# Spreading a block's operand splits by due time, and preparing the second part's first block inside the first part

## The chip, the cores and the metric

The kernel runs on one core of one Trainium2 chip. The metric is the time of one execution on the device in microseconds. The core has five engines with instruction queues of their own: TensorE (PE, with its weight loads as PEld), VectorE (DVE), ScalarE (ACT), GpSimd (POOL) and SyncE (SP, which here only issues DMAs). DMAs can be issued from SP's, ScalarE's and POOL's queue.

## The reference, cut to what matters

```python
# q, k, v: 8 batches x 8 heads x 576 tokens x 64, fp32; k and v are pooled by 8 along the tokens
k_p, v_p = mean over 8 tokens of k, v                   # 72 keys per head
attn = softmax(q @ k_p.T / 8);  o = attn @ v_p          # 8 x 8 x 576 x 64
x = o.transpose(0, 2, 1, 3).reshape(4608, 512)
h = x @ w_in                                            # 512 -> 2048
g = h if h >= 1, 0 if h <= -1, else (h + 1)**2 / 4
x2 = g @ w_out                                          # 2048 -> 512
h = x2 @ w_in2                                          # 512 -> 2048
out = (h - tanh(h)) @ w_out2                            # 2048 -> 512, out is 4608 x 512
```

Each fp32 matrix is cut into a high part, rounded to TensorE's fp32r, and a low part, the remainder. A product is the sum of three: high by high, low by high, high by low. "A split" below is the pair of instructions that makes both parts: ScalarE copies the high part, VectorE subtracts it from the source for the low part.

## The kernel before, in words

The program has two parts.

**Part 1** does the attention and the first layer, in 12 blocks of 384 tokens. Each block has 16 steps (one for each 128 of the 2048 columns). In a step TensorE does the h products of step t and the output products of step t-2; ScalarE and VectorE compute g and split it. Between them stand the pieces of the attention for the next block: queries times keys, the softmax, its transposition (`at_pe`), the copies of the transposed probabilities from PSUM (`at_evac`, `at_evac_a`) and the product with the values (`pv`, L547 to L550). A plan (`add(t, slot, fn)`) says at which step a piece stands in the program; the framework's scheduler then orders each engine's instructions by readiness, with program order as priority. The pooled sequence has 72 keys, 64 + 8 per head: `ah` and `al` hold the 64 of two heads (128 rows), and the remainders of 8 go to `ar`. `at_evac_a` copies them, for each of the block's three token tiles, as one piece of 32 rows (L521) and one of 16 rows (L522). The plan also prepares the second layer's weights (`w2_conv`, `w2_sums`, `w2_own`, `w2_mixed`, 16 units, one per 128 columns): converted, combined into the sums that part 2 needs (four on POOL, L241 to L250), split (L253 on ScalarE, L254 on VectorE) and written to DRAM as `w2c` and `w2o`. Part 1's output goes to DRAM as `x2d`, with stores at L645: on SP's queue, those of the last block on ScalarE's.

**Part 2** does the second layer by Strassen-Winograd: 2 x 2 quarters of each matrix and 7 products in place of 8. It runs over 5 blocks J of 768, 1024, 1024, 1024 and 768 tokens. For each block there are 8 pairs of column tiles q; for each the 7 h products (`h_prod`, L966, order 1, 6, 7, 2, 5, 4, 3, into banks bkA, bkX and bkZ) are combined by VectorE (v_w L995, v_t L998, c22 L1002, c21 L1006, c12 L1009), ScalarE takes tanh (L1013), and g = h - tanh(h) is made in halves by POOL and VectorE (L1017). Two pairs form a group k; the group's operands for the output products are sums of g (`g_s1` to `g_s4`, POOL, L1028 to L1039), split by ScalarE (L1049) and VectorE (L1054). Seven output products (`o_prod`, L1071) follow 8 products behind the h's, VectorE adds each to an accumulator (L1095), and POOL folds the accumulators at a block's end (L1108). The x operands of a block are loaded (`xr_load`, L919), four of the seven are differences (`x_t1` to `x_t4`, POOL, L943 to L953), and all seven are split (`xc_hi` L936 on ScalarE, `xc_lo` L940 on VectorE). The weights come by `wq_load` (L901, nine buffers) and `wo_load` (L906, four buffers) on SP's queue.

In part 2 each engine's order is fixed by hand: `at_time(t, fn, ...)` gives each step a planned time (us, 0 at part 2's first product), computed by a small model of TensorE's time (`ended` of an h product, `began` of an output product), and the steps are emitted in order of these times. The planned times only set the order; what runs when is decided by semaphores. Negative times stand before part 2's first product.

Part 2's buffers lie over part 1's in the same SBUF, slot by slot (`LAYOUT`). A new buffer is placed in the instruction order only after the whole pool of part 1 beneath it is done. Slot r3 (one of the x operands) lay over `sb`, the work buffers that part 1 uses to its last instruction; `half`, a constant of the g computation, lay in the pool `const` with buffers that are done much earlier.

Of the kernel before, what the change touches and what calls it, by code (L numbers as in the profile page):

```python
# [51 lines left out]
def attention_two_moe_kernel(  # L52
# [35 lines left out]
    const = one_pool("const")  # L88
    wpa = one_pool("wpa")
# [18 lines left out]
    ident = const.tile([P, P], F32, tag="ident", name="ident")  # L108
    half = const.tile([P, 1], F32, tag="half", name="half")
    mask = const.tile([P, 2], F32, tag="mask", name="mask")  # L110

    third = const.tile([P, 16], F32, tag="third", name="third")[:, 0:1]
# [398 lines left out]
    def at_evac_a(j, p):  # L511
# [6 lines left out]
        else:  # L518
            for i in range(NTI):
                c = slice(i * P, (i + 1) * P)  # L520
                nc.scalar.activation(ar_t[0:32, c], pr[32 * i : 32 * i + 32], AF.Copy)  # L521
                nc.vector.tensor_copy(ar_t[32:48, c], pr[32 * i : 32 * i + NR])  # L522
# [114 lines left out]
    def out_evac(j):  # L637
        ost = sb.tile([P, KC * TB], F32, tag="ost", name="ost", bufs=1)
        for c in range(KC):
# [5 lines left out]
            (nc.sync if j < NB - 1 else nc.scalar).dma_start(out=x2d[j][c], in_=o)  # L645
# [173 lines left out]
    for f in range(FC):  # L819
# [7 lines left out]
        add(t + 2, "w", w2_sums, f)  # L827
        add(t + 4, "w", w2_own, f)
# [35 lines left out]
    for x in (ps_a, ps_h, ps_o):  # L864
# [11 lines left out]
        "q0 q1 q2 q3 q4 q5 q6 p1664 o0 o1 g0 s0 q7 q8 p2048 x1 x6 r4 o2 o3 r3 g1 k0 k1 th s1 p1024"  # L876
# [64 lines left out]

    def x_t1(J):
        nc.gpsimd.tensor_tensor(XR[(J, 0)], XR[(J, 3)], XR[(J, 0)], ALU.subtract)  # L943

    def x_t3(J):
        nc.gpsimd.tensor_tensor(XR[(J, 3)], XR[(J, 2)], XR[(J, 3)], ALU.subtract)

    def x_t2(J):
        XR[(J, 4)] = two("r4", [P, 2, M2], F32, "xr")[:, :, 0 : half(J)]
        nc.gpsimd.tensor_tensor(XR[(J, 4)], XR[(J, 2)], XR[(J, 0)], ALU.subtract)  # L950

    def x_t4(J):
        nc.gpsimd.tensor_tensor(XR[(J, 1)], XR[(J, 1)], x_src(J, 6), ALU.subtract)  # L953
# [72 lines left out]

    def g_s1(k):
        nc.gpsimd.tensor_tensor(u_of(k, 1), a_of(k, 0, 1), a_of(k, 1, 1), ALU.add)  # L1028

    def g_s2(k):  # L1030
        nc.gpsimd.tensor_tensor(u_of(k, 2), u_of(k, 1), a_of(k, 0, 0), ALU.subtract)  # L1031

    def g_s3(k):
        a = a_of(k, 0, 1)
        nc.gpsimd.tensor_tensor(a, a_of(k, 0, 0), a, ALU.subtract)

    def g_s4(k):
        a = a_of(k, 1, 0)
        nc.gpsimd.tensor_tensor(a, a, u_of(k, 2), ALU.subtract)  # L1039
# [90 lines left out]
    now, ended, began, slots = 0.0, {}, {}, []  # L1130
    LAG = 8
    for s in range(7 * NG + LAG):
        if s < 7 * NG:
            J = s // (7 * NGR)
            for i in (2 * s, 2 * s + 1):
                at_time(now, h_prod, i)
                now += 6 * half(J) * 0.000454
                ended[i] = now
        for n in [s - LAG] if s > LAG + 2 else {LAG + 1: [0], LAG + 2: [1, 2]}.get(s, []):
            k = n // 7  # L1140
            now = max(now, split_at(n) + 2.5)
            at_time(now, o_prod, n)
            began[n] = now
            now += 6 * (half(k // NGR) // P) * 0.1185
            at_time(now + 0.1, add_up, n)
    for i in range(14 * NG):
        at_time((-60 if i < 7 else -18) + i if i < NQ else ended[i - NQ] + 0.05, wq_load, i)
    for n in range(7 * NG):
        at_time((-55 + n, -55 + n, -26, -25)[(n + 2) % 4] if n < NO else began[n - NO] + 3, wo_load, n)
# [5 lines left out]
    for q in range(2 * NG):  # L1155
# [12 lines left out]
        if q % 2:  # L1168
# [6 lines left out]
            at_time(t + 8.1 * r if k == NG - 1 else max(t + 8.1 * r, began[7 * k + 2]), g_s4, k)  # L1175
    for J in range(NJ):
# [4 lines left out]
        steps = (  # L1181
            (e[1], xc_hi, 1), (e[1] + 1.1, xc_lo, 1),
            (e[1] + 2.6, x_t1), (e[1] + 5.2, x_t2), (e[1] + 7.8, x_t3),
            (max(e[6], e[1] + 7.9), xc_hi, 6), (max(e[6], e[1] + 7.9) + 1.1, xc_lo, 6),
# [47 lines left out]
```

## Time and profile before

| what | value |
|---|---|
| median of 3 runs | 1802.79 us (1800.83 to 1806.29) |
| profiled execution | 1803.29 us, span 1801.5 us |
| mean granted TensorE clock | 0.982 |
| TensorE busy | 1705.1 us, 95% |
| VectorE busy | 1240.5 us, 69% |
| ScalarE busy | 844.5 us, 47% |
| POOL busy | 706.2 us, 39% |

The span runs from the first to the last instruction of the profiled execution. Part 1 fills it up to 1015.6 us, when the first matmul of L966 starts; part 2 is the rest. Busy time is that of instructions that compute; a TensorE that is busy at clock 0.5 does half as much. The four block switches of part 2 lie around 1130, 1286, 1454 and 1624 us.

### The profile page before, as it was taken

The page shows a single profiled execution, that of the slowest core. Times are in us where ns is not written, and L with a number is a line of the kernel's source. Part 1 is how long each engine was busy: PE and PEld are TensorE (multiplying, and loading weights), DVE is VectorE, ACT ScalarE, POOL GpSimd, SP SyncE. Part 2 cuts the span into 40 slices and gives each one's busy share as a digit, 9 for nine tenths or more (in the row PEclk, how much of TensorE's full clock was granted, in tenths as well). Part 3 has the DMA queues.
Part 4 walks back from the last instruction along what each step waited for, and adds up shares of the span by engine and source line. Part 5 has one row for each costly group of instructions (what it writes and reads, how often), then busy time and mean ns, then how long its engine had stood idle before and what let it go on. Part 6 is the DMA issues. An engine that isn't in the chain of part 4 may idle for free. (4 is left out here: it accounts for less than half of the span.)

```text
span 1801.5 us, 28136 instructions
## 1 busy us (share of the span) xinstructions
PE 1705.1 (95%) x10176; PEld 1591.5 (88%) x10176; DVE 1240.5 (69%) x1797; ACT 844.5 (47%) x1842; POOL 706.2 (39%) x589
## 2 busy tenths in 40 slices
PE   8999989999989999899999899899899989998997
PEld 6569989899989999898999899799789978998996
DVE  8877766666757676766554457856875787578575
ACT  6656545455545455555443344353435344433442
POOL 5441243321434322432001045644564466446344
PEclk9999999999999999999999999999999999998999
DMA  8631243523434233433101478577556756664873
GB/s 253 224 105 31 68 144 94 150 63 110 136 101 123 89 120 91 144 97 102 27 27 44 154 230 291 171 227 234 167 182 210 234 153 219 199 209 149 285 228 123
DMA packets 220538, 270.56 MB, mean 150 GB/s; under 512 B 82672, under 2 KB 152304, under 8 KB 220400
## 3 DMA queue, kind: packets, MB, share of 16 engines
q1 hardware_dynamic: 219824, 267.98, 47.6%
q8 instruction: 81, 1.33, 0.3%
q10 hardware_dynamic: 576, 0.79, 0.1%
q14 instruction: 57, 0.47, 0.1%
HBM read 219.94 MB, written 48.23 MB: 149 GB/s over the span
## 5 line engine op out<-in xcount | busy, mean ns | idle before, releaser
L1071 PEld LDWEIGHTS ob<-wo,sp 128*128 128x128 f32 x3024 | 384.9, 193 | 32.8 <-DVE sp L1054 16.0
L1071 PE MATMUL ob<-wo,sp 128*128 128x256 f32 x3024 | 392.4, 285 | 20.8 <-DVE sp L1054 13.0
L601 ACT ACTIVATE g<-g,half 128x384 f32<-128x384 f32 x192 | 118.7, 618 | 219.7 <-DVE g L597 219.0
L1017 POOL TENSOR_TENSOR g<-g,th 128x1024 f32<-128x1024 f32 (+1 forms) x40 | 91.7, 2293 | 311.5 <-ACT th L1013 204.6
L635 PE MATMUL po<-gh,whl 128*128 128x384 f32 x704 | 200.0, 345 | 0.0
L966 PE MATMUL bkX<-xc,wq 128*128 128x512 f32 (+1 forms) x720 | 175.4, 380 | 25.1 <-DVE g L1009 15.4
L590 PE MATMUL ph<-xh,whl 128*128 128x384 f32 x704 | 197.0, 341 | 0.8 <-DVE g L605 0.8
L614 DVE TENSOR_TENSOR gl<-g,gh 128x384 fp32r<-128x384 f32 x176 | 118.1, 671 | 77.7 <-ACT gh L613 75.3
L966 PEld LDWEIGHTS bkX<-xc,wq 128*128 128x128 f32 x720 | 131.2, 193 | 44.7 <-DVE g L1009 17.4
L1054 DVE TENSOR_TENSOR sp<-g,sp 128x1024 fp32r<-128x1024 f32 (+1 forms) x100 | 149.8, 1498 | 27.1 <-ACT sp L1049 27.1
L1013 ACT ACTIVATE th<-g 128x1024 f32<-128x1024 f32 (+1 forms) x80 | 78.0, 975 | 191.2 <-DVE g L1006 112.8
L605 DVE TENSOR_TENSOR g<-ph,g 128x384 f32<-128x384 f32 x192 | 106.7, 556 | 81.0 <-ACT g L601 80.0
L478 POOL TENSOR_TENSOR ex<-ex,rc 128x432 f32<-128x432 f32 x44 | 44.0, 999 | 301.8 <-DVE rc L473 154.6
L597 DVE TENSOR_SCALAR g<-ph 128x384 f32<-128x384 f32 x192 | 106.0, 552 | 64.7 <-PE ph L590 58.4
L1095 DVE TENSOR_TENSOR ac<-ob,ac 128x1024 f32<-128x1024 f32 (+1 forms) x110 | 122.2, 1111 | 35.2 <-PE ob L1071 34.9
L613 ACT ACTIVATE gh<-g 128x384 fp32r<-128x384 f32 x176 | 91.5, 520 | 100.8 <-PE po L635 53.7
L1049 ACT ACTIVATE sp<-g 128x1024 fp32r<-128x1024 f32 (+1 forms) x100 | 97.0, 970 | 81.6 <-PE ob L1071 49.2
L635 PEld LDWEIGHTS po<-gh,whl 128*128 128x128 f32 x704 | 131.7, 192 | 0.0
L590 PEld LDWEIGHTS ph<-xh,whl 128*128 128x128 f32 x704 | 128.6, 188 | 2.0 <-DVE g L605 1.7
L590 PE MATMUL ph<-xh,wh 128*128 128x384 f32 x352 | 121.0, 344 | 4.4 <-DVE g L605 4.4
L635 PE MATMUL po<-gh,wh 128*128 128x384 f32 x352 | 123.0, 350 | 0.0
L635 PE MATMUL po<-gl,wh 128*128 128x384 f32 x352 | 121.4, 345 | 0.0
(166 smaller groups left out, 3878.8 us busy)
## 6 DMA issues: line engine op xcount, KB each, us to landing
wq<-w2c SPq DMA_DIRECT2D x280, 256.0 KB, 3.6
wo<-w2o SPq DMA_DIRECT2D x140, 512.0 KB, 3.6
wraw<-in_moe_w_in_dram SPq DMA_DIRECT2D x32, 512.0 KB, 4.0
wraw<-in_moe_w_out_dram SPq DMA_DIRECT2D x32, 512.0 KB, 4.7
out_dram<-ac SPq DMA_DIRECT2D x72, 128.0 KB, 1.8
x2d<-ost SPq DMA_DIRECT2D x44, 192.0 KB, 1.9
w2c<-wraw SPq DMA_DIRECT2D x16, 512.0 KB, 2.9
w2o<-wraw SPq DMA_DIRECT2D x16, 512.0 KB, 2.8
```

Source lines behind the costliest of these rows:

```text
L590: nc.tensor.matmul(ps, a[:, cs], x[:, c, :], start=(i == 0), stop=(i == 3 * KC - 1))
L597: nc.vector.tensor_scalar(a, hp[t], -1.0, 1.0, ALU.max, ALU.min)
L601: nc.scalar.activation(a, a, AF.Square, bias=half, scale=0.5)
L605: nc.vector.tensor_tensor(a, hp.pop(t), a, ALU.max)
L614: nc.vector.tensor_tensor(gl, a, gh.bitcast(F32), ALU.subtract)
L635: nc.tensor.matmul(o, a, m, start=(f == 0 and i == 0), stop=(f == FC - 1 and i == len(ops) - 1))
L966: nc.tensor.matmul(o, w[:, wi, c], x[:, xi, c], start=new and n == 0, stop=n == 5, skip_group_check=not new)
L1017: eng.tensor_tensor(g_of(q, i), g_of(q, i), SN.pop((q, i)), ALU.subtract)
L1049: nc.scalar.activation(x[:, 0, :, 0 : half(k // NGR)], o_src(k, OORD[mi]), AF.Copy)
L1054: nc.vector.tensor_tensor(x[:, 1], o_src(k, OORD[mi]), x[:, 0].bitcast(F32), ALU.subtract)
L1071: nc.tensor.matmul(o[:, c], x[:, xi, p, c * P : (c + 1) * P], w[:, p, wi], start=new and first, stop=True, skip_group_check=not (new and f ...
L1095: nc.vector.tensor_tensor(a, o, a, ALU.add)
```

## The change

- `at_evac_a`: the three 16-row copies of the remainders go from VectorE to ScalarE, so that all six stand there.
- The plan for the second layer's weights: `w2_sums` stands two steps later (t+4 for t+2), `w2_own` one step later (t+5 for t+4).
- The constants `ident`, `half`, `mask` and `third` get a pool of their own, `keep`; in `LAYOUT`, r3 and the pair q5, q6 change places, so r3 no longer lies over `sb`. The first five loads of wq and the third of wo are planned 54 to 60 us before part 2, the sixth and seventh of wq just before it (-2 and -1), the fourth of wo at -0.5.
- The last block's stores of `x2d` are issued from POOL's queue instead of ScalarE's.
- Part 2's first block: `x_t1` to `x_t4` run on VectorE instead of POOL (`x_eng`), and its splits are planned from -34 to -15.
- The other blocks: the low splits of x get times from the table `lo` (us after the first product's operand is free), limited by 4 us before the first product that uses them; `x_t1` to `x_t4` follow the split of x1.
- The end: three output products stand among the last 14 h products instead of seven, and the sums of the last group (`summer`) run on VectorE instead of POOL.

```diff
...
     const = one_pool("const")
+    keep = one_pool("keep")
     wpa = one_pool("wpa")
...
...
     ars = [const.tile([P, TB], F32R, tag=f"ar{i}", name=f"ar{i}") for i in range(2)]
-    ident = const.tile([P, P], F32, tag="ident", name="ident")
-    half = const.tile([P, 1], F32, tag="half", name="half")
-    mask = const.tile([P, 2], F32, tag="mask", name="mask")
-
-    third = const.tile([P, 16], F32, tag="third", name="third")[:, 0:1]
+    ident = keep.tile([P, P], F32, tag="ident", name="ident")
+    half = keep.tile([P, 1], F32, tag="half", name="half")
+    mask = keep.tile([P, 2], F32, tag="mask", name="mask")
+
+    third = keep.tile([P, 16], F32, tag="third", name="third")[:, 0:1]
 
...
...
                 nc.scalar.activation(ar_t[0:32, c], pr[32 * i : 32 * i + 32], AF.Copy)
-                nc.vector.tensor_copy(ar_t[32:48, c], pr[32 * i : 32 * i + NR])
+                nc.scalar.activation(ar_t[32:48, c], pr[32 * i : 32 * i + NR], AF.Copy)
             nc.scalar.activation(ah, pm, AF.Copy)
...
...
                 nc.scalar.activation(o, po[c][:, 0:TB], AF.Copy)
-            (nc.sync if j < NB - 1 else nc.scalar).dma_start(out=x2d[j][c], in_=o)
+            (nc.sync if j < NB - 1 else nc.gpsimd).dma_start(out=x2d[j][c], in_=o)
 
...
...
         add(t + 2, "w", w2_conv, f, 1)
-        add(t + 2, "w", w2_sums, f)
-        add(t + 4, "w", w2_own, f)
+        add(t + 4, "w", w2_sums, f)
+        add(t + 5, "w", w2_own, f)
         add(t + 6, "w", w2_mixed, f)
...
...
     LAYOUT = (
-        "q0 q1 q2 q3 q4 q5 q6 p1664 o0 o1 g0 s0 q7 q8 p2048 x1 x6 r4 o2 o3 r3 g1 k0 k1 th s1 p1024"
+        "q0 q1 q2 q3 q4 r3 p1664 o0 o1 g0 s0 q7 q8 p2048 x1 x6 r4 o2 o3 q5 q6 g1 k0 k1 th s1 p1024"
         " r0 r1 r2 z0 p1728 aS aX a11 a12 a21 a22 u1 u2 x7 x2 x5 x4 x3"
...
...
 
+    def x_eng(J):
+        return nc.gpsimd if J else nc.vector
+
     def x_t1(J):
-        nc.gpsimd.tensor_tensor(XR[(J, 0)], XR[(J, 3)], XR[(J, 0)], ALU.subtract)
+        x_eng(J).tensor_tensor(XR[(J, 0)], XR[(J, 3)], XR[(J, 0)], ALU.subtract)
 
     def x_t3(J):
-        nc.gpsimd.tensor_tensor(XR[(J, 3)], XR[(J, 2)], XR[(J, 3)], ALU.subtract)
+        x_eng(J).tensor_tensor(XR[(J, 3)], XR[(J, 2)], XR[(J, 3)], ALU.subtract)
 
...
         XR[(J, 4)] = two("r4", [P, 2, M2], F32, "xr")[:, :, 0 : half(J)]
-        nc.gpsimd.tensor_tensor(XR[(J, 4)], XR[(J, 2)], XR[(J, 0)], ALU.subtract)
+        x_eng(J).tensor_tensor(XR[(J, 4)], XR[(J, 2)], XR[(J, 0)], ALU.subtract)
 
     def x_t4(J):
-        nc.gpsimd.tensor_tensor(XR[(J, 1)], XR[(J, 1)], x_src(J, 6), ALU.subtract)
+        x_eng(J).tensor_tensor(XR[(J, 1)], XR[(J, 1)], x_src(J, 6), ALU.subtract)
 
...
...
 
+    def summer(k):
+        return nc.vector if k == NG - 1 else nc.gpsimd
+
     def g_s1(k):
-        nc.gpsimd.tensor_tensor(u_of(k, 1), a_of(k, 0, 1), a_of(k, 1, 1), ALU.add)
+        summer(k).tensor_tensor(u_of(k, 1), a_of(k, 0, 1), a_of(k, 1, 1), ALU.add)
 
     def g_s2(k):
-        nc.gpsimd.tensor_tensor(u_of(k, 2), u_of(k, 1), a_of(k, 0, 0), ALU.subtract)
+        summer(k).tensor_tensor(u_of(k, 2), u_of(k, 1), a_of(k, 0, 0), ALU.subtract)
 
...
         a = a_of(k, 0, 1)
-        nc.gpsimd.tensor_tensor(a, a_of(k, 0, 0), a, ALU.subtract)
+        summer(k).tensor_tensor(a, a_of(k, 0, 0), a, ALU.subtract)
 
...
         a = a_of(k, 1, 0)
-        nc.gpsimd.tensor_tensor(a, a, u_of(k, 2), ALU.subtract)
+        summer(k).tensor_tensor(a, a, u_of(k, 2), ALU.subtract)
 
...
...
     NG = NJ * NGR
-    now, ended, began, slots = 0.0, {}, {}, []
     LAG = 8
-    for s in range(7 * NG + LAG):
-        if s < 7 * NG:
-            J = s // (7 * NGR)
-            for i in (2 * s, 2 * s + 1):
-                at_time(now, h_prod, i)
-                now += 6 * half(J) * 0.000454
-                ended[i] = now
-        for n in [s - LAG] if s > LAG + 2 else {LAG + 1: [0], LAG + 2: [1, 2]}.get(s, []):
-            k = n // 7
-            now = max(now, split_at(n) + 2.5)
-            at_time(now, o_prod, n)
-            began[n] = now
-            now += 6 * (half(k // NGR) // P) * 0.1185
-            at_time(now + 0.1, add_up, n)
+    now, ended, began = 0.0, {}, {}
+    seq = []
+    for s in range(7 * NG):
+        seq += [("h", 2 * s), ("h", 2 * s + 1)]
+        n = s - LAG
+        seq += [("o", i) for i in ([n] if n > 2 else {1: [0], 2: [1, 2]}.get(n, []))]
+    late_o = [x for x in seq[-21:] if x[0] == "o"]
+    seq = [x for x in seq if x not in late_o]
+    for i, x in enumerate(late_o[:3]):
+        seq.insert(len(seq) - 10 + 4 * i - i, x)
+    seq += late_o[3:] + [("o", n) for n in range(7 * NG - LAG, 7 * NG)]
+    for kind, i in seq:
+        if kind == "h":
+            at_time(now, h_prod, i)
+            now += 6 * half(i // (14 * NGR)) * 0.000454
+            ended[i] = now
+        else:
+            now = max(now, split_at(i) + 2.5)
+            at_time(now, o_prod, i)
+            began[i] = now
+            now += 6 * (half(i // (7 * NGR)) // P) * 0.1185
+            at_time(now + 0.1, add_up, i)
     for i in range(14 * NG):
-        at_time((-60 if i < 7 else -18) + i if i < NQ else ended[i - NQ] + 0.05, wq_load, i)
+        at_time((-60 if i < 5 else -7 if i < 7 else -18) + i if i < NQ else ended[i - NQ] + 0.05, wq_load, i)
     for n in range(7 * NG):
-        at_time((-55 + n, -55 + n, -26, -25)[(n + 2) % 4] if n < NO else began[n - NO] + 3, wo_load, n)
+        at_time((-26, -25, -54, -0.5)[n] if n < NO else began[n - NO] + 3, wo_load, n)
         k, mi = divmod(n, 7)
...
...
             at_time(t + 5.4 * r, g_s3, k)
-            at_time(t + 8.1 * r if k == NG - 1 else max(t + 8.1 * r, began[7 * k + 2]), g_s4, k)
+            at_time(max(t + 8.1 * r, began[7 * k + 2] - (3.5 * r if k == NG - 1 else 0)), g_s4, k)
     for J in range(NJ):
...
         e = {m: ended[last + i] + 0.05 if J else -34 + 2 * i for i, m in enumerate(HORD)}
-        steps = (
-            (e[1], xc_hi, 1), (e[1] + 1.1, xc_lo, 1),
-            (e[1] + 2.6, x_t1), (e[1] + 5.2, x_t2), (e[1] + 7.8, x_t3),
-            (max(e[6], e[1] + 7.9), xc_hi, 6), (max(e[6], e[1] + 7.9) + 1.1, xc_lo, 6),
-            (max(e[7], e[1] + 10.5), xc_hi, 7), (max(e[7], e[1] + 10.5) + 1.1, xc_lo, 7),
-            (e[2] + 0.2, xc_hi, 2), (e[2] + 1.3, xc_lo, 2),
-            (max(e[2] + 2.6, e[1] + 10.5), x_t4),
-            (e[5], xc_hi, 5), (e[5] + 1.1, xc_lo, 5),
-            (max(e[4], e[1] + 13.3), xc_hi, 4), (max(e[4], e[1] + 13.3) + 1.1, xc_lo, 4),
-            (e[3], xc_hi, 3), (e[3] + 1.1, xc_lo, 3),
-        )
-        for t, fn, *a in steps:
-            at_time(t, fn, J, *a)
+        lo = {1: 2.6, 6: 10.6, 2: 12.6, 7: 15.6, 5: 21.6, 4: 25.6, 3: 29.6}
+        for m, d in lo.items():
+            due = ended[7 * NPR * J + HORD.index(m)] - 4
+            t = max(e[m] + 1.2, min(e[1] + d, due)) if J else e[m] + 1.2 + (6 if m in (6, 7, 4) else 0)
+            at_time(t - 1.2, xc_hi, J, m)
+            at_time(t, xc_lo, J, m)
+            lo[m] = t
+        at_time(lo[1] + 1.4, x_t1, J)
+        at_time(lo[1] + 3.9, x_t2, J)
+        at_time(lo[1] + 6.4, x_t3, J)
+        at_time(max(lo[2] + 1.4, lo[1] + 9), x_t4, J)
         o = 7 * (NGR * (J + 1) - 1)
...
```

## Rows read from the trace of the kernel before

**Rows 1.** Waits of TensorE, whole span: us in total, times, longest us.
```profile
...
PE ppv L549 <- DVE ar L522: 22.3, 20, 4.2
PE bkX L966 <- DVE g L1009: 15.4, 7, 4.2
...
PE bkX L966 <- issue: 6.3, 1, 6.3
...
PE bkA L966 <- DMA wq<-w2c: 3.3, 1, 3.3
...
```

**Rows 2.** Windows by stage: length, busy us (instructions) per engine, TensorE clock, DMA, GB/s.
```profile
...
110.00:1015.00 905.00, 873.07 (x5023) 846.44 (x5022) 594.89 (x1123) 448.88 (x1262) 257.77 (x359) 0.98 0.30 90
1015.00:1056.00 41.00, 33.55 (x190) 31.23 (x189) 21.62 (x29) 18.35 (x28) 12.74 (x7) 0.96 0.79 265
...
1112.00:1166.00 54.00, 46.01 (x279) 41.39 (x278) 46.99 (x42) 23.29 (x32) 39.09 (x16) 0.94 0.56 169
1166.00:1268.00 102.00, 102.00 (x652) 92.59 (x652) 66.40 (x64) 43.64 (x51) 43.88 (x17) 1.00 0.74 236
1268.00:1332.00 64.00, 54.20 (x336) 47.75 (x335) 55.42 (x42) 26.03 (x30) 44.45 (x16) 1.00 0.49 145
...
1438.00:1502.00 64.00, 55.66 (x334) 49.16 (x333) 55.40 (x42) 25.74 (x30) 44.70 (x16) 0.97 0.49 146
...
1608.00:1668.00 60.00, 52.73 (x330) 49.78 (x329) 49.32 (x42) 23.63 (x31) 41.86 (x16) 0.91 0.53 160
...
1758.00:1801.50 43.50, 30.18 (x209) 28.28 (x207) 23.80 (x25) 9.56 (x12) 18.85 (x9) 0.92 0.39 121
...
```

**Rows 3.** Timeline around 260: start, duration, instruction, [idle before, releaser].
```profile
...
258.79 0.25 ACT L521 ACTIVATE ar<-par 32x128 fp32r<-32x128 f32 x1
...
259.82 0.27 ACT L521 ACTIVATE ar<-par 32x128 fp32r<-32x128 f32 x1 [0.78 <-DVE ar L522]
259.99 1.04 ACT L253 ACTIVATE wraw<-wraw 128x1024 fp32r<-128x1024 f32 x1
...
262.32 0.29 DVE L522 CAST ar<-par 16x128 fp32r<-16x128 f32 x1
...
262.66 0.69 PE L549 MATMUL ppv<-ar,vlr 128*128 128x384 f32 x1 [3.18 <-DVE ar L522]
...
```

**Rows 4.** Windows of four short stretches.
```profile
...
260.00:280.00 20.00, 17.34 (x88) 17.21 (x89) 11.80 (x21) 8.54 (x27) 6.24 (x10) 0.83 0.48 148
280.00:300.00 20.00, 20.00 (x121) 19.59 (x120) 13.57 (x26) 10.37 (x31) 6.23 (x10) 1.00 0.17 44
940.00:960.00 20.00, 20.00 (x117) 20.00 (x116) 9.07 (x17) 5.97 (x11) 0.00 (x0) 1.00 0.39 134
1288.00:1300.00 12.00, 8.81 (x52) 7.45 (x53) 12.00 (x11) 4.54 (x6) 1.90 (x1) 1.00 0.44 131
...
```

**Rows 5.** Timeline at 254.8, VectorE.
```profile
...
254.80 1.23 DVE L254 TENSOR_TENSOR wf<-wf,wraw 128x1024 fp32r<-128x1024 f32 x1 [5.30 <-POOL wraw L245]
...
```

**Rows 6.** Timeline of SP's DMA queue: the loads of wq.
```profile
...
954.61 63.94 SPq L901 DMA_DIRECT2D wq<-w2c  x7
...
```

**Rows 7.** Timeline of the second block switch: VectorE and POOL.
```profile
...
1292.64 1.21 DVE L940 TENSOR_TENSOR xc<-xr,xc 128x1024 fp32r<-128x1024 f32 x1
...
1300.76 2.41 POOL L1017 TENSOR_TENSOR g<-g,th 128x1024 f32<-128x1024 f32 x1 [10.87 <-DVE xc L940]
...
1304.30 2.47 DVE L1054 TENSOR_TENSOR sp<-g,sp 128x1024 fp32r<-128x1024 f32 x1 [1.84 <-ACT sp L1049]
...
```

**Rows 8.** Waits of TensorE in the last 43.5 us.
```profile
...
PE ob L1071 <- ACT sp L1049: 4.8, 3, 1.7
PE ob L1071 <- DVE sp L1054: 1.7, 2, 1.4
...
```

**Rows 9.** Lines of the last 43.5 us: count, busy us, mean ns, idle before.
```profile
...
L1017 DVE TENSOR_TENSOR g<-g,th 128x768 f32<-128x768 f32 x1 | 1.0, 959 | 0.5 <-ACT th L1013 0.5
...
```

**Rows 10.** Timeline of the end.
```profile
...
1794.47 2.38 PE L1071 MATMUL ob<-wo,sp 128*128 128x256 f32 x18 [1.65 <-DMA wo<-w2o]
...
```

## The prediction, made before the changed kernel was run

> **What bounds the kernel now.** TensorE is the busiest engine in every stretch, so the question is what it waits for, and where. First its waits over the whole span [rows 1]: the largest is the attention product of L549 waiting for VectorE's `ar` copies, 22.3 us in 20 waits; then bank bkX waiting for c12 (L1009), 15.4 us in 7; one wait of 6.3 us that no event in the profile explains; one of 3.3 for a weight DMA. Then the span by stages [rows 2]. In a steady stretch (1166 to 1268) TensorE is busy for all 102 us at clock 1.00: nothing is to be won there. The idle lies in part 1 (905 - 873.1 = 31.9 us), at the transition (7.5 of 41), at the four block switches (8.0, 9.8, 8.3, 7.3) and in the last 43.5 us (13.3). One column more counts, the granted clock. It steps between two levels, 1.2 and 2.4 GHz, so that 0.83 over 20 us is 2 x 0.17 x 20 = 6.8 us at the lower one and 3.4 us of full-speed work lost; in these rows it is under 1.00 where there are holes, and 1.00 in the steady stretch.
>
> **Part 1, the `ar` copies (A).** Each attention piece from the third block on copies three 32-row pieces on ScalarE and three 16-row pieces on VectorE, by turns, into one tile, and the two engines hand the work back and forth. One of the worst cases [rows 3]: ScalarE's second copy starts at 259.82, then comes a split of the second layer's weights (1.04 us); VectorE's last copy starts only at 262.32; TensorE has by then stood still for 3.18 us. Six copies on ScalarE need no partner. 259.82 to 259.99 is a pitch of 0.17 us, so six take 6 x 0.17 = 1.0 us, or 6 x 0.27 = 1.6 if they don't overlap. Begun with the first at 258.79 they end between 259.8 and 260.4. TensorE arrived at 262.66 - 3.18 = 259.48 and would wait some 0.7 us: 2.5 of 3.18 saved, 78%. Of 22.3 us that is 17. ScalarE gets three copies more in each of 40 evacuations, 120 x 0.27 = 32 us; it is busy for 449 of part 1's 905 us [rows 2], so its idle time hides them, and VectorE is rid of 120 x 0.29. If that cover fails, the copies stand behind a ScalarE instruction of 1.04 us on each of 20 occasions, and 20 us less a rest come back; I bound that at 13.
> The clock: part 1's mean is 0.98 [rows 2], a shortfall of 905 x 0.02 = 18 us. The window with the wait above has 0.83 and 88 matmuls, the next one 1.00 and 121 [rows 4]. I take back under half, 8; the bounds are 0 and 16. A is -25, from -4 (17 - 13) to -33.
>
> **The second layer's preparation, POOL's sums two steps later, the split one.** The scheduler orders part 1's instructions by readiness, with program order as priority, so the shift removes nothing; it can change what VectorE is queued behind. One row shows the risk: L254 at 254.80 came after 5.30 us of VectorE idle, waiting for POOL's sum [rows 5]. The split is now one step behind the sums, not two. I take 0, with -2 and +6 as bounds (one more such event, priced in rival 4); more of it is that rival.
>
> **The transition (B).** On SP's queue seven loads of wq stretch over 63.94 us [rows 6], from 954.6 to 1018.6, past the end of part 1. So TensorE waits 3.3 us for wq [rows 1], and 4.2 us more of idle lie in the stretch from 1015 to 1056 [rows 2]. With part 1's constants in a pool of their own and the slots exchanged, xr3, the first five wq and the splits of block 0 find their room before part 1 ends, and part 1's last stores go from ScalarE's queue to POOL's. I take the 3.3, half of the 4.2 (the rest is the first groups' own splits), and 0.04 x 41 = 1.6 of clock: -7, from -3 (the wq alone) to -9. What moves into part 1's end is seven hi splits on ScalarE, seven lo splits and four x_t on VectorE; 11 at 1.21, the time of one undisturbed [rows 7], are 13 us. From 940 to 960 VectorE is busy 9.07 of 20 us, ScalarE 5.97 and POOL not at all [rows 4], and three such windows follow: hidden. Without that cover each late operand costs its 1.2 us. POOL's queue holds nothing else that the stores could delay.
>
> **The block switches (C).** Five lo splits of the new block, 1.21 us each, stand in VectorE's queue ahead of the c12 that frees bkX; VectorE is busy for all 12 us from 1288 to 1300 [rows 4]. The change spreads them: those of x7, x5, x4 and x3 are put 15.6, 21.6, 25.6 and 29.6 us after the first product, or 4 us before their own product if that is sooner. What goes: the wait of 6.3 us, which stands at the first switch, and about half of the 15.4 for c12, 7.7; the other half, the longest of 4.2 in it, falls later, at the folds, and stays [rows 1]. That is 14. What comes: late splits no longer run beside an idle POOL. POOL stood idle for 10.87 us while such splits ran at 1.21; with its sums begun, a split of the same size took 2.47 [rows 7]. Three splits, four switches, 1.26 us each make 15 us more of VectorE, of which I put a quarter on the path, 4. C is -10. The bounds: three quarters of the idle, 33.4 us, with a fifth of the clock's 0.06 x 54 + 0.03 x 64 + 0.09 x 60 = 10.5 us, -27; and +2.
> By the Trainium skill, page "SBUF — State Buffer", section "Who interferes with whom", a VectorE instruction with two SBUF inputs contends with a GpSimd instruction that reads SBUF, and whichever starts first holds the shared port for its whole length. The 1.21 and 2.47 us agree. If every late split were blocked so, and each had someone waiting, C would be about +1.
>
> **The end (D).** Three output products are kept back, so that 12 and not 9 of them follow the last h product, and the last group's sums go from POOL to VectorE, where an operation of that shape takes 0.959 us [rows 9]. The idle of 13.3 us holds the 4.7 us behind the last product (1801.5 - 1794.47 - 2.38) [rows 10], which stay, and 4.8 and 1.7 us of waiting for the last splits [rows 8], which three products of 2.38 us can cover. 6.5 less a rest of 1, and the clock's 0.08 x 43.5 = 3.5: D is -9, from -3 to -11. VectorE is busy for 23.8 of 43.5 us there [rows 2], so 4 x 0.96 more find room. Late next is the wo load of the last product, 1.65 us [rows 10].
>
> **The sum.** -25 - 7 - 10 - 9 = -51. The profiled execution took 1803.3 us, 1.8 more than its span and half a us above the median of 1802.8; 1803.3 - 51 = 1752.
>
> **The rivals.**
> 1. Late splits are blocked by POOL and C is worth nothing (+1, so 11 more): 1763. For it: VectorE has no slack at a switch [rows 4]. Against it: a late lo costs only when TensorE reaches its product, and the due times leave 4 us.
> 2. The six copies queue on ScalarE behind its other work: of A only -9 remains, 1768. For it: the 1.04 us split in just that place [rows 3]. Against it: ScalarE is half idle.
> 3. The change doesn't do what it says at the transition: loads and splits still come after part 1's last instruction, since a slot's wait holds them. B is nothing, 1759. For it: a queue has stood there for most of 64 us [rows 6], and another could. Against it: VectorE and POOL have the time [rows 4].
> 4. The other side: the second layer's split comes so close behind POOL's sums that VectorE stands still, as at 254.80 [rows 5], in most of the 16 units, with g and TensorE's next product queued behind it. The price: 121 - 88 = 33 matmuls lost [rows 4] at 20 / 121 us, 5.5 us an event. It decides from 51 / 5.5 = 10 units on; in all 16, with A's gain of waits gone as well (the window is of both), 88 - 34 = +54, that is 1857. Against it: order is by readiness, and the priority of what else is ready is untouched.
>
> **How the numbers follow.** Forecast 0.55, rivals 0.20, 0.12, 0.07 and 0.06. The forecast's own range is 1736 to 1768. Were every part at its low end, -33 - 9 - 27 - 11 = -80 gives 1723; at the high ends, -4 - 3 + 2 - 3 = -8, 1795. All ends at once are unlikely: I give 1726 to 1786, with about a tenth above, rival 4 and failures of A together with C, and a tenth below. About 0.3%, 5.4 us, is what a measurement of this kernel can tell from no change. Forecast and rivals 1 to 3 are faster by more than that, 0.94, less 0.02 for several of them together; of rival 4 some comes to rest near zero. Faster 0.92, same 0.03, slower 0.05.
>
> **What would show it.** A: the wait of L549 for `ar` under 8 us, and ScalarE its releaser; part 1 over by about 991 instead of 1015.6. B: no wait for wq at the transition, the first h products without a hole. C: the wait for c12 under 10 us, the 6.3 gone, lo splits beside POOL's sums at 2.4 us. D: the waits for splits at the end under 2. It is wrong if VectorE's waits for POOL at L254 grow severalfold, or if the switches keep 8 us each under a new wait, for operands of x.

## The result, and the profile after

The changed kernel takes 1787.3 us (median of 4, 1786.8 to 1788.7) against 1804.5 us; the ratio is 0.9908, 95% interval 0.9887 to 0.9928. It is faster, as forecast, but by 17 us and not by 51, and the time lies just above the range given (1726 to 1786).

Where the 16 us of the two profiled executions lie (span 1801.5 and 1785.6): the marks are the starts of ScalarE's g activation in part 1 (L601 before, L602 after, 192 of them) and of its c11 copy in part 2 (L992 and L996, one for each of the 40 pairs q); one line of before can sit one to seven lines lower after.

| stretch | before | after | difference | forecast |
|---|---|---|---|---|
| start to the first activation | 41.1 | 45.0 | +3.9 | 0 |
| first to last activation of part 1 | 969.1 | 952.0 | -17.1 | -25 |
| from there to the c11 of q = 4 (transition) | 67.2 | 59.2 | -8.0 | -7 |
| to q = 12, 20, 28, 36 (one block switch in each) | 145.5, 169.6, 169.6, 153.9 | 149.0, 170.8, 170.8, 153.2 | +3.5, +1.2, +1.2, -0.7 | -10 |
| q = 36 to the end | 85.6 | 85.6 | 0 | -9 |

The first row is scatter: in the profiles of the 15 kernels here, whose start is the same work, it lies between 40.8 and 45.0. The second row scatters too. In nine of these profiles (the changed kernel, e3, e4, e5, e7, e8, e9, e11 and e13) VectorE, ScalarE and POOL run part 1 in the same order to the last instruction; TensorE's idle is 20.0 to 23.3 us in them, but the stretch takes 950.9 to 963.5 us. What differs most is the clock: (1 - granted clock) times length, added up over windows of 20 us from 110 on, comes to 6.8 us in the changed kernel's profile and to 17.4 in that of e7. So a difference of some us in the length of part 1 between two profiles says little by itself.

TensorE's waits over the whole span of the changed kernel, against [rows 1]:

```profile
PE ob L1078 <- DVE sp L1061: 15.7, 10, 2.7
PE bkX L970 <- DVE g L1013: 11.1, 5, 4.4
PE psc L450 <- ACT kt L377: 7.5, 8, 2.0
PE ppv L548 <- DVE al L530: 6.5, 5, 2.6
...
PE ppv L551 <- DVE al L530: 3.9, 3, 1.3
PE bkZ L970 <- DVE xc L941: 3.5, 2, 2.0
PE bkX L970 <- DVE xc L941: 2.3, 1, 2.3
...
PE ppv L548 <- ACT ar L523: 2.5, 3, 1.2
```

The waits for `ar`, 22.8 us in all before, are down to 3.3, and the 3.3 for wq and the 6.3 without a releaser are gone. But names that hardly stood in the list of before now hold as much: al 10.4 us at the product with the values, kt 7.5, xc 5.8. Windows of the changed kernel, columns as in [rows 2]; the first is part 1, the second a short stretch in it, the third the transition, four of them the switches, the last the end:

```profile
110.00:997.00 887.00, 863.69 (x5006) 835.17 (x5005) 557.75 (x1012) 487.35 (x1385) 249.27 (x355) 0.99 0.32 97
260.00:280.00 20.00, 17.37 (x101) 16.35 (x100) 12.87 (x24) 11.41 (x36) 8.52 (x13) 1.00 0.43 136
1002.00:1040.00 38.00, 35.69 (x225) 34.83 (x224) 18.74 (x26) 17.19 (x27) 16.79 (x11) 1.00 0.73 229
1100.00:1150.00 50.00, 39.64 (x229) 34.03 (x228) 44.89 (x36) 19.40 (x25) 31.86 (x13) 0.97 0.51 151
1250.00:1316.00 66.00, 57.76 (x341) 51.09 (x340) 58.60 (x43) 25.96 (x30) 46.50 (x16) 0.95 0.51 155
1420.00:1486.00 66.00, 57.70 (x345) 51.30 (x344) 58.62 (x44) 26.03 (x30) 46.48 (x16) 0.95 0.51 153
1592.00:1652.00 60.00, 53.30 (x336) 50.56 (x336) 52.83 (x42) 24.36 (x31) 43.08 (x16) 0.91 0.53 161
1742.00:1785.60 43.60, 30.14 (x223) 28.72 (x222) 28.71 (x31) 9.91 (x12) 11.10 (x5) 0.96 0.44 133
```

TensorE's idle: part 1 23.3 us (31.9 before), the switches 10.4, 8.2, 8.3 and 6.7 (8.0, 9.8, 8.3, 7.3), the end 13.5 (13.3). Only the transition became what was forecast: 2.3 us of idle and clock 1.00. At the second switch the idle fell, from 9.8 to 8.2 us, and the stretch is longer even so: the granted clock is 1.00 there in [rows 2] and 0.95 now, which is 0.05 x 66 = 3.3 us of full-speed work.

### The profile page after: what moved, and what is told of

It is laid out like the page before. It is cut to its first block, busy times and chain, and to the rows that moved or that the text cites. A ratio compares the mean times of both kernels' runs of the same rounds, so it can differ in the third digit from the quotient of the medians.

```text
span 1785.6 us, 28158 instructions
## 1 busy us (share of the span) xinstructions
PE 1699.8 (95%) x10176; PEld 1586.3 (89%) x10176; DVE 1214.3 (68%) x1685; ACT 880.1 (49%) x1962; POOL 695.2 (39%) x585
## 5 line engine op out<-in xcount | busy, mean ns | idle before, releaser
L602 ACT ACTIVATE g<-g,half 128x384 f32<-128x384 f32 x192 | 118.7, 618 | 183.5 <-DVE g L598 181.6
L970 PE MATMUL bkX<-xc,wq 128*128 128x512 f32 (+1 forms) x720 | 175.9, 380 | 15.9 <-DVE g L1013 11.1
L615 DVE TENSOR_TENSOR gl<-g,gh 128x384 fp32r<-128x384 f32 x176 | 109.1, 620 | 88.3 <-ACT gh L614 87.3
L328 POOL TENSOR_TENSOR kvraw<-kvraw 128x768 f32<-128x768 f32 (+2 forms) x84 | 111.1, 1322 | 23.0 <-DMA kvraw<-in_v_dram 16.4
```

What stands on the lines that cost most here:

```text
L328: eng.tensor_tensor(a[..., 0:n], a[..., 0:n], a[..., n : 2 * n], ALU.add)
L602: nc.scalar.activation(a, a, AF.Square, bias=half, scale=0.5)
L615: nc.vector.tensor_tensor(gl, a, gh.bitcast(F32), ALU.subtract)
L970: nc.tensor.matmul(o, w[:, wi, c], x[:, xi, c], start=new and n == 0, stop=n == 5, skip_group_check=not new)
```

## The experiments

Each was timed in rounds with the kernel before on the same chip. Ratios are to the kernel before; the changed kernel has 0.9908, and 0.001 is 1.8 us.

| run | median us | ratio, 95% interval |
|---|---|---|
| e1 copies back on two engines | 1797.8 | 0.9964 [0.9949, 0.9978] |
| e2 preparation's slots back | 1788.2 | 0.9911 [0.9892, 0.9929] |
| e3 splits' old times | 1781.6 | 0.9871 [0.9851, 0.9891] |
| e4 old end | 1782.7 | 0.9885 [0.9863, 0.9907] |
| e5 additions first at the end | 1783.1 | 0.9887 [0.9866, 0.9907] |
| e6 POOL's sums left out | 1761.3 | 0.9765 [0.9743, 0.9787] |
| e7 quiet POOL at the switches | 1771.8 | 0.9818 [0.9794, 0.9842] |
| e8 the same, splits' old times | 1772.8 | 0.9820 [0.9801, 0.9839] |
| e9 preparation spaced out | 1786.6 | 0.9901 [0.9882, 0.9919] |
| e10 sums on VectorE | 1775.9 | 0.9834 [0.9811, 0.9857] |
| e11 end mended | 1783.2 | 0.9879 [0.9858, 0.9901] |
| e12 e3, e10 and e11 together | 1770.6 | 0.9815 [0.9790, 0.9841] |
| e13 first switch earlier | 1786.4 | 0.9886 [0.9866, 0.9906] |

### Part 1: e1, e2, e6, e9, e10

The edit of e1, and what was expected:

```diff
-                nc.scalar.activation(ar_t[32:48, c], pr[32 * i : 32 * i + NR], AF.Copy)
+                nc.vector.tensor_copy(ar_t[32:48, c], pr[32 * i : 32 * i + NR])
```

> The changed kernel with the three 16-row copies of ar back on VectorE; all else as changed (1787.3 us). Theory (the copies on one engine are what made part 1 shorter; what is left of TensorE's idle there has other causes): about 1802, with 15 to 22 us of waits of TensorE for ar back and part 1 over near 1017. Rival (the copies only moved the wait to ScalarE's queue, and most of the 17 us of part 1 come from the preparation's two later slots): about 1791.

It came in between, 10 us above the changed kernel and, with the old copies, still 7 below the kernel before; no run says what those 7 are. In its profile TensorE waits 16.1 us for `ar` again, and, as in the changed kernel, 10.4 for al: the waits for al do not come from the copies. Its part 1 takes 963.7 us (952.0), as long as that of e7, so the copies' worth rests on the medians and on the waits.

```diff
-        add(t + 4, "w", w2_sums, f)
-        add(t + 5, "w", w2_own, f)
+        add(t + 2, "w", w2_sums, f)
+        add(t + 4, "w", w2_own, f)
```

> The changed kernel with w2_sums back at t+2 and w2_own at t+4; all else as changed (1787.3 us). Theory (the split one step behind the sums makes VectorE wait about 2 us in each of the 16 units with al queued behind it, and TensorE's 10.4 us of waits for al come from that): about 1778, the waits for al under 2 us. Rival (six copies in a row on ScalarE, with ah and kt behind them, cause these waits): 1787 within 3, the waits for al still 8 or more.

No difference. The waits for al did go (0.7 us), but others took their place: g 6.2, the softmax's rr on POOL 6.1, `ar` 7.1. TensorE's waits in part 1 by what was waited for, in us, with two runs that follow:

| waited for | before | changed | e1 | e2 | e6 | e10 |
|---|---|---|---|---|---|---|
| `ar` | 22.8 | 3.3 | 16.6 | 7.1 | 2.6 | 2.9 |
| al | 0.9 | 11.1 | 10.4 | 0.7 | 2.8 | 1.2 |
| kt (ScalarE's queue) | 0 | 7.1 | 0 | 2.7 | 5.9 | 11.2 |
| g | 5.2 | 0.8 | 0 | 6.2 | 0.4 | 1.2 |
| rr | 1.9 | 0.8 | 0 | 6.1 | 0 | 0 |
| idle in all | 31.9 | 23.3 | 27.7 | 25.7 | 12.0 | 16.5 |

The waits for al come with the new slots (changed kernel and e1), those for kt with the copies on ScalarE (all but before and e1). So the slots decide who stands in VectorE's queue. What it stands behind is seen in the changed kernel at 345.55, where the longest wait for al ended (timeline, ScalarE, VectorE and TensorE):

```profile
341.54 0.48 ACT L524 ACTIVATE ah<-pam 128x384 fp32r<-128x384 f32 x1
...
342.87 1.23 DVE L255 TENSOR_TENSOR wf<-wf,wraw 128x1024 fp32r<-128x1024 f32 x1 [2.33 <-POOL wraw L246]
...
344.94 0.55 DVE L530 TENSOR_TENSOR al<-pam,ah 128x384 fp32r<-128x384 f32 x1
...
345.55 0.36 PE L548 MATMUL ppv<-ah,vh 128*128 128x192 f32 x1 [2.60 <-DVE al L530]
```

ScalarE had made ah by 342.0. VectorE could have made al at once, but its queue's head was the split of the second layer's weights, which waited 2.33 us for POOL's sum and then took 1.23; two more operations of 0.55 us stood between it and al. VectorE waits like this in all 16 units, and did so before as well, 32.2 us both times. VectorE's waits, first of the changed kernel, then of the one before:

```profile
DVE wf L255 <- POOL wraw L246: 16.8, 8, 2.3
DVE wf L255 <- POOL wraw L251: 15.4, 8, 2.0
```

```profile
DVE wf L254 <- POOL wraw L245: 24.9, 8, 5.3
...
DVE wf L254 <- POOL wraw L250: 7.3, 8, 1.8
```

e6 takes the sums away (the line `add(t + 4, "w", w2_sums, f)` is left out):

> The changed kernel with POOL's four sums per unit of the second layer's weights left out (64 operations; the mixed weights are then wrong, the rest of the work is the same). Theory (in part 1 al waits in VectorE's queue behind the split that waits 2 us for these sums, 32 us of VectorE in all, and TensorE's 10.4 us of waits for al come from there): about 1777, no wait for al over 0.5. Rival (the six copies in a row on ScalarE, before which ah stands, make al late): 1786, the waits for al as before.

26 us, more than twice what was expected; the waits for al went down to 2.8 us, not to nothing (longest 1.0). Part 1 takes 935.2 us in a profile that is the longest of the five runs; its idle is 12.0 us and its clock 1.00. e10 keeps the sums and moves all eight lines of them to the engine that waits for them:

```diff
-            nc.gpsimd.tensor_tensor(c1, a12, a11, ALU.subtract)
+            nc.vector.tensor_tensor(c1, a12, a11, ALU.subtract)
...
```

> The changed kernel with the four sums per unit on VectorE instead of POOL (64 operations of 128 x 256, about 0.35 us each by the ratio of widths to its 1.23 us for 1024, 22 us more of VectorE). Theory (not the sums' work but VectorE's wait for the other engine is what costs; leaving the sums out gave 26 us): 1768, no wait of VectorE for POOL at the split. Rival (VectorE's queue is what al and g stand in, and 1.4 us more per unit cost as much as the wait): 1787 or above.

1775.9, 11 us less, with 35 us more work on VectorE (an addition of 128 x 256 took 0.41 us in the median and 0.55 on the mean, not the 0.35 estimated). That lies between theory and rival, and VectorE no longer waits for POOL at the split. So the wait for the other engine cost more than the work. Both e6 and e10 also rid POOL of the sums; that this alone made part 1 shorter was not tested, but of TensorE's waits in the changed kernel's part 1 only 0.8 us are for POOL. TensorE's waits in part 1 (110 to 990) of e10:

```profile
PE psc L450 <- ACT kt L377: 11.2, 8, 1.9
PE ppv L550 <- ACT ar L523: 1.6, 4, 0.6
...
PE ppv L551 <- DVE al L530: 0.3, 2, 0.2
PE ppv L548 <- DVE al L530: 0.2, 1, 0.2
```

al is almost gone; what shows next is ScalarE's kt. e9 only moved the slots apart (sums t+3, split t+6, mixed split t+7):

> The changed kernel (1787.3 us) with the second layer's preparation spaced out: sums at t+3, the split three steps behind them at t+6, the mixed split at t+7. Theory (VectorE waits for POOL's sums because the split stands only one step behind them): the 32 us of that wait fall to a third, 1779. Rival (the split is taken up as soon as the sums are near, whatever its slot, or the sums cost through POOL's queue, where the softmax stands behind them): 1787 within 3, the waits for al and for rr as large as before together.

As the rival said: 1786.6, and VectorE's wait is 16.8 + 15.4 us, to the tenth that of the changed kernel. But the edit moved nothing: in both profiles VectorE, ScalarE and POOL run part 1 in the same order. So e9 shows only that these slots leave the scheduler's order as it is; what a split further behind its sums would bring stays untested. The slots of e2 did change the order, and there VectorE waits 22.7 + 15.4 us.

### The block switches: e3, e7, e8, e13

e3 keeps the old list of `steps` for J > 0 and the new times for J = 0.

> The changed kernel with the splits of x of blocks 2 to 5 planned as before the change; the first block's as changed (1787.3 us). Theory (the spread costs 3 us at the first switch, where TensorE then waits for xc itself, and about 1 at the second and third, because the late splits run beside POOL's sums): about 1782, the first switch back to the hole of 6 us without a named releaser and without waits for xc. Rival (the spread gained its 10 us and the switches lost as much to something else in the change): about 1797.

As the theory said. The four stretches are 145.6, 169.7, 169.8 and 154.0 us again, 639.1 in all, against 643.7 with the spread and 638.5 before. The first of these differences is in every profile: with the spread the first stretch takes 148.9 or 149.0 us in all nine that have it unaltered. The second is not: there the second stretch takes 169.2 or 169.3 in five of the nine, no more than before, and 170.8 in four. VectorE's lines between q = 12 and q = 20, first of the changed kernel, then of e3 (count, busy us, mean ns):

```profile
L1061 DVE TENSOR_TENSOR sp<-u,sp 128x1024 fp32r<-128x1024 f32 x8 | 17.0, 2126 | 8.0 <-ACT sp L1056 7.9
L941 DVE TENSOR_TENSOR xc<-xr,xc 128x1024 fp32r<-128x1024 f32 x7 | 13.9, 1990 | 4.2 <-ACT xc L937 4.2
```

```profile
L1061 DVE TENSOR_TENSOR sp<-u,sp 128x1024 fp32r<-128x1024 f32 x8 | 16.0, 1998 | 10.2 <-ACT sp L1056 10.2
...
L941 DVE TENSOR_TENSOR xc<-xr,xc 128x1024 fp32r<-128x1024 f32 x7 | 10.7, 1533 | 3.3 <-ACT xc L937 3.3
```

The same seven splits take 13.9 us instead of 10.7 when they are spread. The timeline of the second switch of the changed kernel shows beside what (VectorE and POOL):

```profile
1285.66 3.25 POOL L1038 TENSOR_TENSOR u<-u,g 128x1024 f32<-128x1024 f32 x1
1288.87 3.39 POOL L1042 TENSOR_TENSOR g<-g 128x1024 f32<-128x1024 f32 x1
```

```profile
1287.73 2.27 DVE L941 TENSOR_TENSOR xc<-xr,xc 128x1024 fp32r<-128x1024 f32 x1
1290.04 3.31 DVE L1061 TENSOR_TENSOR sp<-u,sp 128x1024 fp32r<-128x1024 f32 x1
```

Each of the two splits ends 1.1 us behind the POOL operation that ran when it started (1290.00 behind 1288.91, 1293.35 behind 1292.26), and that is about what such a split takes alone, 1.21 us in [rows 7].

e7 and e8 take most of POOL's reads for the sums away at the end of the first four blocks, with the spread and without (g_s2 likewise writes u2, and g_s3 returns at once; g_s4, POOL's half of g and the folds stay):

```diff
     def g_s1(k):
+        if last_of_block(k):
+            return nc.gpsimd.memset(u_of(k, 1), 0.0)
...
```

> The changed kernel; at the end of each of the first four blocks POOL's first two sums of the last group are memsets and the third is left out, so POOL reads no SBUF there until the folds (the sums are then wrong). To be compared with the next run, which has the splits' old times. Theory (the late splits lose to POOL's reads: lo splits of 1.99 us on the mean against 1.53): the splits of x at about 1.3, this run some 8 below the changed kernel, near 1779, and not slower than the next one. Rival (the splits are late by their own due times, POOL has no part): 1785, and 5 or 6 slower than the next one.

> The kernel with the old times of the splits of x in blocks 2 to 5 (1781.6), with the same memsets in place of POOL's sums at the end of the first four blocks. Theory: the old times had kept the splits clear of POOL's sums, so only the operands' splits of the output products gain: about 1779. Rival: the same 1779, with the run before 5 or 6 above it.

With so quiet a POOL the spread costs nothing: 0.9818 and 0.9820; the four stretches are 625.3 and 626.0 us, and VectorE's work from q = 12 to 20 is 126.1 and 126.0 us (130.9 and 128.6 with POOL's sums). TensorE's idle in the four stretches is 19.6 us with the spread and 23.1 without; with POOL's sums it is 33.6 (changed kernel) and 33.1 (e3). So the spread's price hangs on POOL's sums. Both runs also came out 6 to 7 us below what was expected: the memsets are shorter than the sums, 0.96 us against 2.4 and more, so everything behind them is earlier too, and the two runs do not part this from the reads. The theory missed in another detail: the spread splits of e7 still take 1.84 us on the mean, not 1.3; what remains beside them of POOL (the memsets, g_s4, its half of g, the folds) was not taken apart.

The first switch is a case of its own: 3.5 us lost, and there TensorE waits for xc itself. e13 changes its due times alone:

```diff
-            due = ended[7 * NPR * J + HORD.index(m)] - 4
+            due = ended[7 * NPR * J + HORD.index(m)] - (8 if J == 1 else 4)
```

> The changed kernel (1787.3 us) with the limit of the splits' planned times 8 us instead of 4 before the end of the first product that uses them, at the first switch alone: there the splits of x6, x7, x5, x4 and x3 move forward by 1.1, 2.5, 3.6, 4.0 and 4.0 us, nothing else changes. Theory (at the first switch, where the block before is smaller and the uses come 5 to 7 us sooner after the first product than at the second, the fixed times leave too little ahead of a queue that runs late: TensorE's 6.4 us of waits for xc there): the waits for xc under 2 us, the stretch of that switch 3 us shorter, 1784. Rival (the splits come late because each is stretched by POOL's reads, whatever their place): the waits for xc stay, 1787.

TensorE's waits from 1094 to 1146 of e13:

```profile
PE ob L1078 <- DVE sp L1061: 4.6, 4, 2.1
PE bkX L970 <- ACT sp L1056: 1.9, 1, 1.9
PE bkX L970 <- DVE g L1013: 0.4, 1, 0.4
```

No wait for xc is left, and the stretch to q = 12 is 145.1 us, 3.9 less (3.4 us of such waits were left in e7, with POOL quiet). The median does not show it (1786.4, six runs from 1780.8 to 1789.9); the ratio, 0.9886, is 4 us lower, with intervals that overlap. The stage settles the cause, the whole time does not confirm its size.

### The end: e4, e5, e11

e4 goes back to one output product after each pair of h products up to the last, and to POOL's sums in the last group.

> The changed kernel with the end's order and the last group's sums (POOL) as before the change (1787.3 us). Theory (the end is set by a cycle of four steps per output product, hi, lo, the addition behind it on VectorE, the next product, which three more products only lengthen): 1787 within 2, idle of TensorE in the last 43 us about 8.6 as before. Rival (the kept back products do cover the splits, and something else in the changed kernel takes 9 us back): about 1796.

1782.7: both were off; the end's change may have cost something. In the profile q = 36 to the end is 84.3 us instead of 85.6; most of the rest of the 4.6 lies in the start and in part 1, which the edit does not touch. But the same old end took 85.6 us in the kernel before, the changed end takes 85.3 to 87.9 in the ten profiles that have it, and the intervals of the two ratios overlap: a cost of the end's change is not shown, only that it gained nothing. How the end of the changed kernel runs, VectorE and TensorE:

```profile
1758.02 0.96 DVE L1061 TENSOR_TENSOR sp<-g,sp 128x768 fp32r<-128x768 f32 x1 [1.96 <-ACT sp L1056]
1758.90 0.95 DVE L1042 TENSOR_TENSOR g<-g 128x768 f32<-128x768 f32 x1
1759.77 0.95 DVE L1102 TENSOR_TENSOR ac<-ob,ac 128x768 f32<-128x768 f32 x1
1760.64 0.95 DVE L1061 TENSOR_TENSOR sp<-u,sp 128x768 fp32r<-128x768 f32 x1
1760.82 4.55 PE L1078 MATMUL ob<-wo,sp 128*128 128x256 f32 x36 [1.22 <-ACT sp L1056]
```

The product at 1760.82 has its operand by 1758.98, yet it starts only behind the addition of 1759.77, which ends at 1760.72 (the row names ScalarE's split that ended at 1760.53, but that is the next product's): an output product writes the bank that the product two before it left, so that one's addition must have read it. And the addition stands in VectorE's queue behind the low split, which waits for ScalarE, which waits for the operand's buffer; of these there are two. Product, hi, lo, one of the sums that moved here, addition, next product: that is a circle, and a product kept back is itself a part of it. e5 puts the additions first:

```diff
-        at_time(t + 1.1 * r, sp_lo, n)
+        lo_t = t + 1.1 * r
+        if n >= 7 * NG - 12:
+            lo_t = max(lo_t, began[n - 2] + 6 * (half(k // NGR) // P) * 0.1185 + 0.12)
+        at_time(lo_t, sp_lo, n)
```

> The changed kernel (1787.3 us) with one order changed at the end: for the last 12 output products, VectorE's addition of product n stands ahead of the low split of product n+2, not behind it. Theory (the end is set by a cycle: product n ends, hi, lo, then the addition, and only then product n+2): about 1782, the idle of TensorE in the last 43 us down from 8.5 to 4 or less. Rival (hi and lo, which wait for the operand's buffer, set the pace, wherever the addition stands): 1787 within 2, with waits for the low split of the same 8 us.

In e5 the last group's fourth sum overwrites an operand before its low split has read it, so its output is wrong. e11 is the same with that sum planned later, at `began[7 * k] + 2.5`.

> The changed kernel with the additions ahead of the low splits for the last 12 output products, and the last group's fourth sum behind the low split that reads its operand (in the run e5_add_first it stood ahead of it, and that split then read the overwritten operand). Theory: 1783, as that run; idle of TensorE in the last 43 us about 4. Rival (that run was faster only because its split did not wait for the sum's order): 1787.

1783.1 and 1783.2; the stretch from q = 36 is 83.4 and 83.6 us, 2 less and below all ten profiles with the changed end, at a lower clock from the last c11 on (0.94 in e11, where the changed kernel has 0.96). Besides the end's own chain, TensorE's idle in the last 43.5 us is 4.4 us in e5 and 6.0 in e11, where the theory had 4. The stretch shows the circle; the whole time agrees, but its intervals overlap with the changed kernel's. TensorE's waits there in e11, and five products in one run:

```profile
PE ob L1078 <- ACT sp L1056: 2.5, 2, 1.4
PE ob L1078 <- DVE sp L1061: 1.8, 3, 1.1
PE ob L1078 <- ACT th L1017: 1.5, 1, 1.5
```

```profile
1752.39 12.29 PE L1078 MATMUL ob<-wo,sp 128*128 128x256 f32 x88 [0.35 <-DVE sp L1061]
```

### All together: e12

> The changed kernel with the three edits that each made it faster: the splits of blocks 2 to 5 at their old times (5.8 less), the sums of the second layer's weights on VectorE (11.4 less), the additions ahead of the low splits at the end (4.1 less). Theory (the three lie in different stretches, part 1, the switches and the end, and add up): 1787.3 - 21.3 = 1766. Rival (the faster part 1 only brings the next stretch's waits forward, so that a half comes back): 1776.

1770.6, between the two: ratio 0.9815 to the kernel before, faster than both kernels. Against the changed kernel's profile part 1 is 9.9 us shorter, the four stretches 4.6, the end 2.0, and the start, which is scatter, 3.5. Its part 2 lost 1.8 at the transition.

## Why the prediction was wrong

The sum was 51 us and 16 came, or 20 without the start's scatter.

- **Part 1's clock, and the copies.** Taken: 17 us of idle and 8 of clock. The idle fell by 8.6, beyond its scatter. For the clock, added up over windows of 20 us from 110 on, 15.6 us before became 6.8, so 8.8 came; but one order of part 1 gave 6.8 to 17.4, so that this term came out is luck as far as one profile of each kernel can tell. The step that failed is "2.5 of 3.18 saved, 78%" as a saving of time: it followed the copies to their end and asked what is late next only for them. The waits for `ar` did fall by 19.5 of 22.8 us. But al came in with 11.1, behind the split of the second layer's weights that waits for POOL's sum, and kt with 7.1, in ScalarE's queue. It comes only where the copies stand on ScalarE, which speaks for rival 2 in part; but just ahead of kt ScalarE's g activation had itself waited for VectorE (1.88 us before 324.77, kt at 326.00). [rows 5] held that wait for POOL, and the prediction used it only for a rival about the slots. It is the likely root of the waits for `ar` too: in 9 of the 22, 14.0 of the 22.8 us, VectorE had waited for POOL at L254 at most 9 us earlier; for the other 13 the trace shows no such wait so near. e6 and e10 put its price in the changed kernel at 26 us without the sums and 11 with them on VectorE.
- **The slots** were put at 0: right for the time (e2). Not for the path: the 10 us of waits for al are theirs, and e2 only exchanges them for others. Rival 4 had its mechanism there, but in all units from the beginning, so the change added none of it (32.2 us of VectorE's waits for POOL before and after).
- **The transition** was right, -7 against -8.0, and the waits for wq are gone as it said. No run takes this part back by itself.
- **The switches.** Taken -10, came +5. The contention was estimated well: 15 us more of VectorE; the sums of its busy times from q = 4 to q = 36 grew by 12.7 us. So was the 4 us of it on the path: at the four switches the waits for VectorE's splits of the output products' operands rose from 9.7 to 14.1 us. The step that failed is the gain of 14. The waits for c12 went only from 15.3 to 11.1, 4.2 and not 7.7 less. And the 6.3 us of the first switch were counted as gained outright. They were c12's too (before, c12 ran from 1135.49 to 1136.03, and the next matmul began at 1136.14), and they did go; but the splits that made room for c12 were then late themselves, and 6.4 us of waits for xc, 0.6 of them for the hi, came in their place, a term that the prediction put at nothing. Its "the due times leave 4 us" counted to the end of the product; by the plan's own model a product takes 1.4 us, so 2.6 were left. In all, TensorE's idle in the four stretches is 33.4 us before and 33.6 after: the waits changed their names, not their sum. Of the 5 us 3.5 are the clock's (10.2 before, 13.7 after), which the -10 also had at nothing; why the clock fell more is open. By the Trainium skill, page "SBUF — State Buffer", section "SBUF: two separate sides", the first to start holds the shared port for the whole instruction. By that rule the prediction made C +1; it measured +5. The 2.27 and 3.31 us beside POOL's 3.25 and 3.39, against 1.21 alone, agree with it, and e7 against e8 shows that the spread is free when three of POOL's four sums are out of its way.
- **The end.** Taken -9, came 0. The step "which three products of 2.38 us can cover" failed: the waits for splits were links of a circle through two buffers, the bank and VectorE's order, not a delay that other work could hide. The idle of the last stretch is 8.6 us besides the end's own chain, 8.7 before.

The range missed by 1.3 us. Three of four parts fell short at once, which was taken to be unlikely. They have one thing in common, the order in VectorE's queue, but no single run shows it for all three.

## What to carry to other kernels

A wait names the operation that came last, not the one that made it late: before an operation is moved away, look at what its queue's head was waiting for, since the next operation in that queue inherits the wait. Work spread out in time on a saturated engine moves beside other work, so the price is that of the new neighbours: compare TensorE's waits as a sum, not by name. At an end without filling work, write down the circle of one item (product, hi, lo, addition, bank) and count its time, before keeping work back to cover it.

## What was not expected of the hardware

- The same busy time at another clock: from 260 to 280 TensorE is busy for 17.34 us before and 17.37 after, with granted clocks of 0.83 and 1.00 and 88 and 101 matmuls [rows 4]. Before, one hole there has 3.18 us; after, the two have 1.21 and 1.29. It is tempting to read from this that small holes cost less clock than one large one. The runs do not bear that out: e7 runs part 1 in the changed kernel's order, with 22.8 us of idle against 23.3 and its longest hole 2.6 us as there, and loses 17.4 us to the clock against 6.8. So much of the clock's cost belongs to the single execution and not to the order of the program.
- POOL is slowed too: its operations of 128 x 1024 took 2.4 us where no split of VectorE's ran beside them [rows 7] and 3.25 to 3.39 beside its splits.
